# Turning rows by 32x32 blocks on VectorE and carrying the blocks by SBUF copies, in an RWKV-5 attention with a SoLU feed-forward

## The chip, the cores and the metric

The kernel runs on one core of a Trainium2 chip. Its five engines work side by side and meet at semaphores: TensorE (PE; its weight loads are shown as PEld), VectorE (DVE), ScalarE (ACT), GpSimd (POOL) and SyncE (SP), which here issues nearly all DMAs. Each engine takes its instructions strictly in the order in which the program lists them. The metric is the device time of one launch in microseconds. The profile is of one execution.

## The reference

Inputs are r, k and v of shape (4 batches, 8 heads, 768 steps, 48), a decay w and a bonus u of shape (8, 48), and the feed-forward weights w_in (384 x 1024) and w_out (1024 x 384), both in 8-byte floats, with a gain g_ln of 1024.

```python
for t in range(S):
    kt, vt, rt = (k[:, :, t], v[:, :, t], r[:, :, t])
    cur = np.einsum('bhd,bhe->bhde', u[None] * kt, vt)
    y[:, :, t] = np.einsum('bhd,bhde->bhe', rt, state + cur)
    state = w[None, :, :, None] * state + np.einsum('bhd,bhe->bhde', kt, vt)
...
h = x @ w_in                       # x: y as 3072 rows of 384
e = np.exp(h - h_max)
solu = h * (e / e.sum())
ln = (solu - mu) / np.sqrt(var + 1e-06) * g_ln
return ln @ w_out
```

## The kernel before

**Units.** The 3072 rows are 24 units of 128 rows, unit i being batch i % 4 and chunk i // 4 of 128 steps. The recurrence is worked by chunks: within a unit as products of r, k and v with a mask, and between the chunks of one batch through a carried state.

**Stages of a unit.** They are functions that each issue instructions on several engines:

- `load(i, "kr")`, `load(i, "v")` bring the rows in (SP). `decay_k`, `decay_r` and `weigh` multiply them with tables of decays on POOL (L722, L729, L735, L736), into `kp`, `rp` and `rku`; `sum_own` sums `rku` on DVE; `diagonal` writes the diagonal of the score matrix `G` on POOL (L755).
- The scores need r and k turned, features on partitions: `rT` and `kT`. Units below 9 (`FIRST`) are turned by TensorE (`turn_r`, `turn_k`). From unit 9 on it goes through a DMA: `halve_k` and `halve_r` split 4-byte words into lower and upper 2-byte halves on ACT (L1038, L1044; a few on DVE), `turn` issues one transposing DMA on SP (L1012), which turns 2-byte elements only, and `join_rk` puts the halves together again on DVE (L1017).
- `attend` multiplies the scores (L820) and the outer products for the state (L903); `place` copies parts of `rT` into `G` on ACT (L772, L773); `take` moves scores and states out of PSUM on DVE (L833, L924); `merged_y` (L876) and `take_y` give the attention's output; `update` carries the state on (DVE L939, then POOL L942).
- `ffn_in` multiplies with w_in (L952) and takes the exponential on ACT (L957). Its PSUM tile `h_ps` is there once, so the next `ffn_in` waits until `unit_a` (DVE L962, L964) has read it. `unit_b` takes the sum of squares on ACT (L972 from unit 4, `SEVEN`, on), `deviation` makes scale and shift of it on POOL (L984 to L992), and `normalise` applies them on ACT (L998).
- The rows must be turned again for w_out, into `lnT`, with the same three steps: `halve_ln` (ACT L1023), the DMA, `join_ln` (DVE L1017).
- The product with w_out is plain for units 0 to 3 (`ffn_out`, L1062). From unit 4 on two units share seven block products instead of eight: `row_sums_12` and `row_sums_34` form sums s1 to s4 of halves of `lnT` (DVE L1097, L1098; DVE or POOL L1102, L1103). `both_a` has three blocks: two from `lnT` itself, one from s2. `both_b` has three, from s1, s3 and s4, and `both_c` one from `lnT` of the second unit. A block is eight matmul instructions (L1107). Two PSUM accumulators are used in turn; between blocks ACT copies (L1124, L1135, L1140, L1166) or DVE adds (L1133, L1151, L1155) must read them. In `both_b` the copy of L1140 stands between the block from s1 and the block from s4, which use the same accumulator.

**Order.** The whole order of work is written out by hand. After a start for units 0 to 2, a loop over i = 2 to 6 does one unit per turn; a stretch for i = 7 follows; then a loop over i = 9, 11, ..., 23 does two units per turn: attention of units i and i+1, the first product of units j = i-2 and j+1, the second product of units l = i-7 and l+1 (by blocks from l = 4 on), and the loads, decays and turns of units ahead. Three last stretches follow, for l = 18, 20 and 22. The weights come as 14 pieces of 8-byte floats, are rebuilt as 4-byte floats in the first loop, and are loaded and examined again later (`check_next`, from i = 15 on) for a flag that chooses a general path, not taken here.

**The turn of rows around the change.** Within a pair's turn POOL begins with `deviation(j - 2, j)`, for the two units of the turn before; then come the diagonals, row_sums_34, and the decays. `normalise`, `halve_ln` and `join_ln` are spread over ACT's and DVE's order one unit at a time. The split halves and the raw weights share six buffers. `lnT` has two buffers, and the last six units use parts of `big`.

Of the kernel before, what the change touches and what calls it, by code (L numbers as in the profile page):

```python
# [399 lines left out]
def direct_path(  # L400
# [29 lines left out]
    nc = tc.nc  # L430
# [10 lines left out]
    LA, LO, FIRST, WHOLE, CHECKED = 2, 5, 9, 4, 15  # L441
    SEVEN, EARLY, ON_ACT = 4, 12, 12
    ROOM = {18: 4, 19: 5, 20: 3, 21: 2, 22: 1, 23: 0}
# [72 lines left out]
    raws = {}  # L516

    def load_weights(j, tag="raw", bufs=6):
        dst, src, _ = pieces[j]
        raws[j] = wpool.tile([128, dst.shape[1], 2], U32, tag=tag, name="raw", bufs=bufs)  # L520
        n = dst.shape[1]
        n = n if tag == "raw" or j >= 5 else n // 2
        for at in range(0, dst.shape[1], n):
            nc.sync.dma_start(out=raws[j].rearrange("p n o -> p (n o)")[:, 2 * at : 2 * (at + n)],
                              in_=src[:, 2 * at : 2 * (at + n)])
# [53 lines left out]
    def check_words(j):  # L579
# [48 lines left out]
    bigs = [const.tile([128, 8 * T], F32, name=f"big{i}") for i in range(6)]  # L628
# [131 lines left out]
    def factors(i):  # L760
        X = live.setdefault(i, {})
        n = TURNED[i % 3] if i < WHOLE else 2 - i % 2
        X["rk"] = bigs[n].rearrange("p (e a t) -> p e a t", e=2, a=HP)
        X["rT"], X["kT"] = X["rk"][:, 0], X["rk"][:, 1]
        return X

    def place(i):

        X = live[i]
        for q in range(2):  # L770
            rows = slice(q * P, q * P + D)
            nc.scalar.copy(out=X["G"][P : P + D, 0, :, q, :], in_=X["rT"][rows, :, 0:U])  # L772
            nc.scalar.copy(out=X["G"][0:D, 1, :, q, :], in_=X["rT"][rows, :, U:T])  # L773
# [33 lines left out]
    def scores(chunks, at=0):  # L807
# [4 lines left out]
        for n, i in enumerate(chunks, at):  # L812
# [3 lines left out]
            for a in range(HP):  # L816
                for c in range(2):
                    for q in range(2):
                        rows = slice(q * P, q * P + D)
                        nc.tensor.matmul(X["scores"][q][ts(c, U), a, :], X["kT"][rows, a, ts(c, U)],  # L820
                                         X["rT"][rows, a, ts(c, U)], start=True, stop=True)
# [179 lines left out]
    def halves():  # L1001

        return wpool.tile([128, 2 * 8 * 64, 1], U32, tag="raw", name="halves",
                          bufs=6).bitcast(U16).rearrange("p n o -> p (n o)")

    def split(words):
        return words.bitcast(U16).rearrange("p (n o) -> p o n", o=2)

    def turn(both):

        turned = halves()
        nc.sync.dma_start(out=turned.rearrange("p (n t) -> p n t", t=128), in_=both,  # L1012
                          transpose=True)
        return turned.rearrange("p (o n t) -> p o n t", o=2, t=128)

    def join(words, turned):
        nc.vector.tensor_copy(out=words.bitcast(U16).rearrange("p n (t o) -> p o n t", o=2),  # L1017
                              in_=turned)

    def halve_ln(i):  # L1020
        X = live[i]
        both = halves()
        nc.scalar.copy(out=both.rearrange("p (o n) -> p o n", o=2), in_=split(X["solu"]))  # L1023
        X["turned"] = turn(both)

    def join_ln(i):
        X = live[i]
        if i not in ROOM:
            X["lnT"] = fpool.tile([128, KF, 128], F32, name="lnT")
        else:  # L1030
            X["lnT"] = bigs[ROOM[i]].rearrange("p (f t) -> p f t", f=KF)
        join(X["lnT"], X["turned"])

    def halve_k(i):
        X = live[i]
        X["both"] = halves()
        parts = X["both"].rearrange("p (o e n) -> p o e n", o=2, e=2)
        nc.scalar.copy(out=parts[:, :, 1], in_=split(X["kp"].rearrange("p h d -> p (h d)")))  # L1038

    def halve_r(i):  # L1040
        X = live[i]
        parts = X["both"].rearrange("p (o e n) -> p o e n", o=2, e=2)
        copy = nc.vector.tensor_copy if i < ON_ACT else nc.scalar.copy
        copy(out=parts[:, :, 0], in_=split(X["rp"].rearrange("p h d -> p (h d)")))  # L1044
        X["turned"] = turn(X["both"])

    def halve_rk(i):
        if FIRST <= i < N:
            halve_k(i)
            halve_r(i)  # L1050

    def join_rk(i):
        X = factors(i)
        join(X["rk"].rearrange("p e a t -> p (e a) t"), X["turned"])
# [34 lines left out]
    def turn_next(i):  # L1089
        normalise(i)  # L1090
        halve_ln(i)
# [186 lines left out]
    for i in range(LA, LA + LO):  # L1278
# [22 lines left out]
        if i - LO >= 0:  # L1301
            halve_ln(i - LO)
        if i - LO - 1 >= 0:
            join_ln(i - LO - 1)
# [22 lines left out]
        halve_rk(i + 3)  # L1327
# [3 lines left out]
    def check_next():  # L1331
        for p in checked:
            check_words(p)
        checked[:] = [checks.pop(0)] if checks else []
        for p in checked:
            load_weights(p, "check", 1)
# [13 lines left out]
    deviation(0, j)  # L1350
    ffn_in(j)
    halve_k(i + 3)
    attend([i + 1], 1)
    unit(j)
    halve_r(i + 3)
    place(i + 1)
    join_ln(l + 1)
# [7 lines left out]
    halve_ln(l + 2)  # L1365
    join_rk(i + 2)
    ffn_out(l)
    load(i + 6, "kr")
    ffn_in(j + 1)
    unit_a(j + 1)  # L1370
# [3 lines left out]
    join_rk(i + 3)  # L1374
# [5 lines left out]
    halve_rk(i + 4)  # L1380
    unit_b(j + 1)
    halve_ln(l + 3)
    normalise(l + 4)
    join_ln(l + 2)
# [3 lines left out]
    for i in range(LA + LO + 2, N, 2):  # L1388
        j, l = i - LA, i - LA - LO
        seven = l >= SEVEN  # L1390
        for n in (i + 6, i + 7):
# [5 lines left out]
        deviation(j - 2, j)  # L1397
        first, second = ([n] if n < N else [] for n in (i + 2, i + 3))
        for n in first + second:
            diagonal(n)  # L1400
# [199 lines left out]
```

## Time and profile before

| what | value |
|---|---|
| median of 3 runs | 326.86 us (326.11 to 326.93) |
| the profiled execution | 325.9 us, span 324.2 us |
| mean granted clock of TensorE | 0.996 |
| ACT splits of solu (L1023), 24 | 45.5 us, 1896 ns each |
| ACT splits of kp and rp (L1038, L1044) | 15.5 and 12.5 us |
| DVE joins (L1017), 21 and 18 | 33.5 and 30.4 us |
| transposing DMAs, 39 | 4.9 us from issue to landing (median) |
| DMA queue of SP | packets take 84.2% of 16 engines' span; 158302 of 165780 packets under 512 B |

The span is the time from the first to the last instruction. Busy time of an engine counts the time in which it works on an instruction, and a group's mean is the time of one instruction. "Idle before" is the time in which the engine had nothing to do ahead of the group, with what ended that wait. The chain of waits starts from the last instruction and goes back, at each step to whatever released it; it shows which work set the time. The timeline gives instructions by their start in the span.

### The profile page before, as it was taken

To read this page: it belongs to the slowest core of one execution; us is meant where nothing else is said; L and a number is where in the kernel's file an instruction comes from. 1 tells how busy PE (TensorE), PEld (TensorE's weight loads), DVE (VectorE), ACT (ScalarE), POOL (GpSimd) and SP (SyncE) were. 2 spreads that over 40 slices of the span, in tenths; PEclk is the share of its full clock that TensorE was granted. 3 is DMA by queue.
4 is the path that set the end of the run, shared out by engine and by line. 5 is a ranking of instruction groups with operands and counts; after the bars stand their busy time and mean duration, and the time that the engine had idled before them with its cause. 6 is when DMAs were issued, how large, how long until landed. Compare 5 with 4: busy or idle time off the path is not lost.

```text
span 324.2 us, 9670 instructions
## 1 busy us (share of the span) xinstructions
PE 311.9 (96%) x3915; PEld 217.4 (67%) x3915; DVE 255.2 (79%) x434; ACT 244.1 (75%) x414; POOL 220.1 (68%) x237
## 2 busy tenths in 40 slices
PE   8999999999999999899999999999999999999993
PEld 6766556555556457477678667668668667678993
DVE  7796999998887979988798587988579675284571
ACT  5876887988469888768968969959967958957520
POOL 5989778799999999999999999969134020131000
PEclk9999999999999999999999999999999999999998
DMA  7999999689999999986998999978993383873621
GB/s 155 231 276 204 200 207 190 109 141 160 199 165 168 181 198 121 163 175 112 167 181 186 180 193 217 199 185 129 182 197 66 90 191 76 149 169 70 174 80 61
DMA packets 165780, 52.62 MB, mean 162 GB/s; under 512 B 158302, under 2 KB 161503, under 8 KB 165727
## 3 DMA queue, kind: packets, MB, share of 16 engines
q1 hardware_dynamic: 165724, 51.92, 84.2%
q8 instruction: 32, 0.52, 0.7%
q14 instruction: 22, 0.17, 0.2%
q10 hardware_dynamic: 2, 0.00, 0.0%
HBM read 26.75 MB, written 4.72 MB: 97 GB/s over the span
## 4 chain that ended last, share of the span: by engine, by line
PE 53%; DVE 16%; POOL 14%; issue 6%; DMA 4%; ACT 4%; SPq 1%; POOLq 0%; DVEq 0%
PE o_ps L1107 24%; PE h_ps L952 20%; PE y_ps L876 4%; DMA rpad<-in_r_dram 4%; POOL rp L729 3%; POOL big L755 3%; POOL kp L722 3%; POOL rku L735 3%; DVE ma L552 2%; DVE big L833 2%; PE at L820 2%; DVE solu L964 2%; DVE ma L550 1%; PE kv_ps L903 1%; POOL rku L736 1%
## 5 line engine op out<-in xcount | busy, mean ns | idle before, releaser
L952 PE MATMUL h_ps<-w_in_sb,xT 128*128 128x512 f32 x288 | 129.7, 599 | 0.2 <-POOL w_in_sb L560 0.2
L952 PEld LDWEIGHTS h_ps<-w_in_sb,xT 128*128 128x128 f32 x288 | 53.1, 190 | 60.7 <-issue 56.6
L1023 ACT COPY halves<-solu 128x2048 uint16<-128x2048 uint16 x24 | 45.5, 1896 | 0.2
L984 POOL TENSOR_SCALAR stats<-stats 128x2 f32<-128x2 f32 (+2 forms) x12 | 6.2, 520 | 49.8 <-ACT e L972 49.3
L1017 DVE COPY lnT<-halves 128x2048 uint16<-128x2048 uint16 x18 | 30.4, 1702 | 6.2 <-DMA halves<-halves 6.2
L957 ACT ACTIVATE e<-h_ps 128x1024 f32<-128x1024 f32 x24 | 24.5, 1021 | 12.8 <-PE h_ps L952 12.6
L722 POOL TENSOR_TENSOR kp<-kpad,kdec 128x512 f32<-128x512 f32 x24 | 32.6, 1360 | 1.9 <-DMA kpad<-in_k_dram 1.3
L1017 DVE COPY big<-halves 128x2048 uint16<-128x2048 uint16 x21 | 33.5, 1599 | 0.3
L964 DVE SCALAR_TENSOR_TENSOR solu<-h_ps,stats,e 128x1024 f32<-128x1024 f32 x24 | 30.8, 1283 | 2.1
L755 POOL TENSOR_SCALAR_AFFINE_SELECT big<-own 64x512 f32<-64x512 f32 x40 | 29.8, 745 | 1.7
L736 POOL TENSOR_TENSOR rku<-rku,rpad 128x384 f32<-128x384 f32 x24 | 29.1, 1214 | 1.9
L833 DVE COPY_PREDICATED big<-later_half,at 64x512 f32<-64x512 uint32 x40 | 29.5, 738 | 0.7
L735 POOL TENSOR_TENSOR rku<-kpad,u_bc 128x384 f32<-128x384 f32 x24 | 29.0, 1210 | 0.1
L1107 PE MATMUL o_ps<-w_out_sb,ma 128*128 128x192 f32 x160 | 28.3, 328 | 0.1
L998 ACT ACTIVATE solu<-solu,stats 128x1024 f32<-128x1024 f32 x20 | 24.7, 1235 | 4.2 <-POOL stats L992 4.2
L942 POOL TENSOR_TENSOR vt<-vt,wide 48x384 f32<-48x384 f32 x16 | 20.2, 1277 | 9.8 <-DVE vt L939 9.2
L1107 PEld LDWEIGHTS o_ps<-w_out_sb,ma 128*128 128x128 f32 x160 | 26.1, 190 | 0.9 <-ACT o L1140 0.4
L962 DVE RECIPROCAL stats<-sums 128x1 f32<-128x1 f32 x24 | 3.8, 156 | 28.5 <-ACT e L957 28.4
L729 POOL TENSOR_TENSOR rp<-rpad,rdec 128x512 f32<-128x512 f32 x15 | 25.2, 1678 | 0.0
L972 ACT ACTIVATE e<-solu,stats 128x1024 f32<-128x1024 f32 x20 | 22.9, 1145 | 1.4 <-DVE solu L964 1.1
L1062 PE MATMUL o_ps<-w_out_sb,lnT 128*128 128x384 f32 x64 | 21.6, 491 | 0.0
L876 PE MATMUL y_ps<-big,vt 128*32 128x64 f32 (+1 forms) x1280 | 20.7, 220 | 0.4 <-issue 0.4
(148 smaller groups left out, 610.9 us busy)
## 6 DMA issues: line engine op xcount, KB each, us to landing
raw<-in_moe_w_out_dram SPq DMA_DIRECT2D x16, 384.0 KB, 3.8
kpad<-in_k_dram SPq DMA_DIRECT2D x24, 192.0 KB, 5.0
rpad<-in_r_dram SPq DMA_DIRECT2D x24, 192.0 KB, 5.3
vt<-in_v_dram SPq DMA_DIRECT2D x40, 96.0 KB, 3.9
out_dram<-o SPq DMA_DIRECT2D x20, 192.0 KB, 3.5
raw<-in_moe_w_in_dram SPq DMA_DIRECT2D x7, 512.0 KB, 6.7
raw<-in_moe_w_in_dram SPq DMA_DIRECT2D x10, 256.0 KB, 3.3
vt<-in_v_dram SPq DMA_DIRECT2D x4, 192.0 KB, 6.7
```

The lines of the kernel that those rows point to most:

```text
L722: nc.gpsimd.tensor_mul(X["kp"].rearrange("p h d -> p (h d)"), kpads[i % NLD].rearrange("p h d -> p (h d)"), kdec.rearrange("p a d -> p (a ...
L729: nc.gpsimd.tensor_mul(X["rp"].rearrange("p h d -> p (h d)"), rpads[i % NLD].rearrange("p h d -> p (h d)"), rdec.rearrange("p a d -> p (a ...
L735: engine.tensor_mul(rku, kpads[i % NLD][:, :, 0:D], u_bc)
L736: engine.tensor_mul(rku, rku, rpads[i % NLD][:, :, 0:D])
L755: nc.gpsimd.affine_select(out=G[rows, c].rearrange("p a q u -> p (a q) u"), in_=X["own"][rows].to_broadcast([U, H, U]), compare_op=ALU.is_ ...
L833: nc.vector.copy_predicated(X["G"][rows, c].rearrange("p a q u -> p q a u"), later_half[rows].unsqueeze(1).to_broadcast([U, 2, HP, U]), X[ ...
L876: nc.tensor.matmul(y_ps[ts(g, 32), j, ts(c, U)], vf[:, at : at + 32], X["G"][rows, c, h // 2, h % 2, :], start=(g not in opened), stop=las ...
L952: nc.tensor.matmul(h_ps[:, ts(n, NX)], X["xT"][:, j, :], w_in_sb[:, j, ts(n, NX)], start=(j == 0), stop=(j == KD - 1))
L964: nc.vector.scalar_tensor_tensor(out=solu, in0=X["h"], scalar=rs, in1=X["e"], op0=ALU.mult, op1=ALU.mult, accum_out=tot)
L1017: nc.vector.tensor_copy(out=words.bitcast(U16).rearrange("p n (t o) -> p o n t", o=2), in_=turned)
L1023: nc.scalar.copy(out=both.rearrange("p (o n) -> p o n", o=2), in_=split(X["solu"]))
L1107: nc.tensor.matmul(dst, rows[:, f], weights[:, f], start=(start and f == 0), stop=(f == KH - 1), skip_group_check=True)
```

## The change

Rows no longer pass through 2-byte halves and the transposing DMA.

- `turn_ln(i)` and `turn_rk(i)` turn 32x32 blocks of 4-byte words with VectorE's transpose: one instruction of 1024 elements a partition for ln, two of 512 for r and k of a unit. A block stays on its 32 partitions. The results go to `block_ln` and `block_rk`.
- `move` carries the blocks between the four groups of 32 partitions by 16 plain SBUF-to-SBUF copies on SP, each 32 partitions by 256 words of one or two units. `move_ln` and `move_rk` do it for two units at once (one at a time for ln of units 0 and 1, and for r and k of unit 23).
- In the new layout consecutive rows (t) of `lnT`, and of r and k from unit 9 on, lie 8 words apart. The scores, `place`, the row sums and the blocks read them so.
- `deviation` now takes units j-1 and j of the same turn, behind `unit_b(j)`; two `normalise` stand around `ffn_in(j + 1)`.
- The raw weights get eight fixed slots, which the blocks and `lnT` use later. The weight check is split into `check_load` and `check_words` and starts at i = 11.
- In the last stretch `row_sums_12` stands behind `both_a`'s first two blocks.

```diff
-    LA, LO, FIRST, WHOLE, CHECKED = 2, 5, 9, 4, 15
-    SEVEN, EARLY, ON_ACT = 4, 12, 12
-    ROOM = {18: 4, 19: 5, 20: 3, 21: 2, 22: 1, 23: 0}
+    LA, LO, FIRST, WHOLE, CHECKED = 2, 5, 9, 4, 11
+    SEVEN, EARLY = 4, 12
...
+    slots = const.tile([128, 8, 8 * T], F32, name="slots")
+    block_ln, rows_ln, block_rk = slots[:, 6:8], (slots[:, 0:2], slots[:, 2:4]), slots[:, 4:6]
...
+            X["rk"] = bigs[n].rearrange("p (g t e a) -> p e a g t", g=4, e=2, a=HP)
+            X["r"], X["k"] = X["rk"][:, 0], X["rk"][:, 1]
...
-                        nc.tensor.matmul(X["scores"][q][ts(c, U), a, :], X["kT"][rows, a, ts(c, U)],
-                                         X["rT"][rows, a, ts(c, U)], start=True, stop=True)
+                        nc.tensor.matmul(X["scores"][q][ts(c, U), a, :], X["k"][rows, a, ts(c, 2)],
+                                         X["r"][rows, a, ts(c, 2)], start=True, stop=True)
...
+    def move(dst, src):
+        for m in range(4):
+            for g in range(4):
+                nc.sync.dma_start(out=dst[ts(m, 32), :, ts(g, 256)], in_=src[ts(g, 32), :, ts(m, 256)])
+
+    def places_ln(i):
+        dst = rows_ln[i // 2 % 2] if i < N - 4 else big[:, 4:6] if i < N - 2 else big[:, 1:3]
+        return block_rk if N - 4 <= i < N - 2 else block_ln, dst
+
+    def turn_ln(i):
+        nc.vector.transpose(
+            out=places_ln(i)[0][:, i % 2].rearrange("p (m t f) -> p f m t", m=4, f=KF),
+            in_=live[i]["solu"].rearrange("p (f m x) -> p f m x", m=4, f=KF))
+
+    def move_ln(i, n=2):
+        src, dst = places_ln(i)
+        for k in range(i, i + n):
+            live[k]["lnT"] = dst[:, k % 2].rearrange("p (m f) -> p f m", f=KF)
+        move(dst[:, i % 2 : i % 2 + n], src[:, i % 2 : i % 2 + n])
+
+    def turn_rk(i):
+        for e, x in enumerate((live[i]["rp"], live[i]["kp"])):
+            nc.vector.transpose(
+                out=block_rk[:, 1 - i % 2].rearrange("p (m t e a) -> p e a m t", m=4, e=2, a=HP)[:, e],
+                in_=x.rearrange("p h d -> p (h d)").rearrange("p (a m x) -> p a m x", a=HP, m=4))
+
+    def move_rk(i):
+        for n in (i, i + 1):
+            if n < N:
+                factors(n)
+        n = min(2, N - i)
+        move(big[:, 1 : 1 + n], block_rk[:, 0:n])
```

The loop over pairs after the change, in its order (calls that stand as before are cut to the names that the text uses):

```python
for i in range(LA + LO + 2, N, 2):
    j, l = i - LA, i - LA - LO
    ...
    for n in first + second:             # units i+2, i+3
        diagonal(n)
    turn_ln(l + 2)
    turn_ln(l + 3)
    if i >= CHECKED:
        check_load()
    move_ln(l + 2)
    for n in first + second:
        turn_rk(n)
    decay(i + 4)
    decay(i + 5)
    if seven:
        row_sums_12(l)
        row_sums_34(l, nc.vector if l > EARLY else nc.gpsimd)
    ...
    ffn_in(j)
    attend([i, i + 1])
    unit_a(j)
    if seven:
        both_a(l)
    ...
    if first:
        move_rk(i + 2)
    unit_b(j)
    deviation(j - 1, j + 1)
    take([i, i + 1])
    ...
    normalise(l + 4)
    ffn_in(j + 1)
    normalise(l + 5)
    if seven:
        both_b(l)
    unit_a(j + 1)
    if seven:
        both_c(l)
    check_least()
    ...
```

Its last stretch:

```diff
     l += 2
-    both_a(l)
+    both_a(l, (0, 1))
     take_a(l, "DVE")
+    row_sums_12(l)
+    both_a(l, (2,))
     take_a(l, "ACT")
-    check_least()
     compare_sums()
     row_sums_34(l, nc.vector)
```

## The prediction

> **What bounds the kernel now.** I read the page's busy times first, then a table of six stretches, then the chain of waits inside one pair of units, then single lines. One number answers most of it:
>
> ```profile
> PE 311.9 (96%) x3915; PEld 217.4 (67%) x3915; DVE 255.2 (79%) x434; ACT 244.1 (75%) x414; POOL 220.1 (68%) x237
> ```
>
> TensorE is busy 311.9 of 324.2 us. Busy can hide waits, so the table by stretches (columns: length, then busy PE, PEld, DVE, ACT, POOL with counts, clock, DMA share, GB/s) says where the other 12.3 us lie:
>
> ```profile
> 0.00:26.00 26.00, 23.45 (x303) 17.23 (x303) 22.17 (x66) 18.26 (x43) 20.55 (x37) 1.00 0.99 214
> 26.00:67.00 41.00, 38.86 (x620) 24.07 (x624) 37.38 (x68) 33.46 (x65) 33.03 (x35) 1.00 0.94 184
> 67.00:136.00 69.00, 67.34 (x831) 38.65 (x831) 60.65 (x81) 55.26 (x82) 66.19 (x63) 1.00 1.02 165
> 136.00:247.00 111.00, 110.61 (x1600) 80.06 (x1601) 90.28 (x139) 89.47 (x144) 92.57 (x89) 1.00 0.91 171
> 247.00:303.00 56.00, 55.42 (x470) 41.79 (x468) 35.49 (x62) 44.64 (x73) 7.75 (x16) 1.00 0.58 123
> 303.00:324.20 21.20, 16.23 (x98) 15.57 (x98) 9.23 (x23) 3.03 (x10) 0.00 (x0) 0.94 0.36 104
> ```
>
> From 26 to 303 us TensorE idles only 2.14 + 1.66 + 0.39 + 0.58 = 4.8 us. That is the most the change can win there. POOL is almost full from 67 to 136 (66.19 of 69). One pair of units, as the chain of waits has it (start, length, what):
>
> ```profile
> 188.84 1.93 PE y_ps L876 x128
> 190.77 5.35 PE h_ps L952 x12
> 196.11 1.09 PE at L820 x64
> 197.21 0.72 PE kv_ps L903 x64
> 197.93 4.10 PE o_ps L1107 x24
> 202.02 0.03 issue
> 202.05 5.42 PE h_ps L952 x12
> 207.47 5.29 PE o_ps L1107 x32
> ```
>
> All TensorE, back to back, some 23.9 us a pair. Relieving other engines is worth nothing here; delaying TensorE costs in full. Call E the end of the third block of both_b (187.3 here; the next is 1.3 before the 5.29 us stretch ends).
>
> **Part by part, removed.** ACT loses its splits: 45.5 us (24 x 1.896), 15.5 and 12.5 us. VectorE loses the joins, 33.5 + 30.4 us, and 39 transposing DMAs go. In the pairs that is hidden behind TensorE already: price 0. Only POOL gains, through the joins:
>
> ```profile
> L729 POOL TENSOR_TENSOR rp<-rpad,rdec x15: 1264/1288/2338, 69.9 to 211.0; 128x512 f32<-128x512 f32 x15
> L722 POOL TENSOR_TENSOR kp<-kpad,kdec x24: 1267/1277/2347, 9.4 to 209.8; 128x512 f32<-128x512 f32 x24
> ```
>
> Equal products take 1.27 us or up to 2.35 (shortest/median/longest). Setting POOL's rows against VectorE's: the 18 kp products with no join beside them average 1.28 us, the 6 with at least 0.4 us of one 1.61 us. POOL's time over its shortest rows sums to 29.7 us, some 21.6 of it where joins (L1017) overlap. What stays after the change is about 8 us. The Trainium skill, "SBUF — State Buffer", section Who interferes with whom, says a VectorE instruction with one SBUF input outside its two-port modes leaves GpSimd alone; no row here shows a turn. By the page the stall worked out below stays at its middle value; if turns were of the two-port kind it would go to its upper one.
>
> **Added.** VectorE turns: per pair two of 1024 elements and four of 512. No row shows a turn. Bounds: a plain pass at one element a step, 1.28 us per 1024 (L964) and 0.69 per 512 (L780); from above twice that, since writes go 32 bytes apart. I take the rows: 2 x 1.28 + 4 x 0.69 = 5.3 us against 4 joins x 1.65 = 6.6. VectorE has room: about E+10 for row_sums_12, when the exponential of the next unit ends.
>
> SyncE issues 16 copies per move, 13 moves for ln and 8 for r, k: 336 issues for 39. The shortest issues of plain DMAs (L1156) take 0.33 us, with 0.08 between: 0.41, so 6.6 us a move. Per pair: 13.1 for two moves, 2.6 for four k, r loads, 2.8 for four v loads, 2 for checks, 1 for results: 21.5 of 23.9 us. It fits, narrowly; at a k load's 0.57 + 0.08 each it is 29.2 and doesn't. I take 0.41: few rows of 1 KB each are nearest to the output's 128 rows. What is queued behind move_rk (it waits for place) are check_load and the results, none due within 5 us.
>
> Strided operands: lnT and r, k are read by TensorE 32 bytes apart. No row of before does that. Lower bound 0. Upper: the transposes of L787 (a 128-column load and a matmul of 128) run 0.11 us apart, so a load takes no more; doubled it is 0.22 against the 0.163 us between matmuls of L1107. 24 per pair x 0.057 x 10 pairs = 13.7 us, and scores (1.09 us per pair) doubled add 0.545 x 15 units = 8.2: 22 us. I take 0, nearest row: VectorE reads 8 bytes apart (L550, 512 words) in 692 ns, a dense pass of 512 (L780) takes 689. The Trainium skill speaks against it: "SBUF — State Buffer", section Door 1: The DMA port swizzle, has 16-byte lines in SBUF and a penalty for each access that enters a new one, which a step of eight f32 always does. By the rule the sum would hold those 22 us, by the rows 0.
>
> Start to 136 us: POOL regains most of its 13.7 us of slow rows there and VectorE two joins, but TensorE idles only 3.8; i = 5 gets a turn of 1.28 us where VectorE is on the chain and had no join, and i = 7 makes POOL wait for the deviation of a unit just computed, with two diagonals and two decays queued behind. I take -1.2 (bounds -3.8, all of that idle time, and +2, one wait for such statistics).
>
> The weight checks stay 14, but run two a pair from i = 11 on: 0.87 us of ACT (L582 with its accumulator) and 0.6 of VectorE (L590) each. ACT hides its part under TensorE now that it has lost some 8 us of splits a pair (two of 1.90, four of 1.04); VectorE's lies ahead of POOL's start and is counted there. Weights landing in fixed slots cost nothing: the same loads, with more room.
>
> **Moved: the deviation.** Before, POOL computes deviation(j-2, j) first in the pair, on old statistics (193.3 us), and normalise runs on ACT in a free place. After, deviation(j-1, j+1) stands behind diagonal, two whole decays and row_sums_34, and normalise(l+4) stands on ACT ahead of the exponential of ffn_in(j+1), normalise(l+5) behind it, then the copy of both_b. That copy frees the accumulator for TensorE's third block of both_b. From E:
> - POOL starts when VectorE has done o, a check_least (0.6) and two updates: E+1.85. Then, at undisturbed rows, two L942 2.0, four L755 2.8, two decays with their products 9.0, row sums 2.5, deviation 1.4: D = E+19.6. Statistics are ready at E+17.1 (place ends E+15.9, Square 1.2), so POOL ends last.
> - ACT after D: normalise 1.13, exponential 1.03, normalise 1.13, copy 0.3: D+3.7.
> - TensorE: ffn_in(j+1) ends at 207.47, E+20.2; after two blocks of 1.3 it wants the copy at E+22.8.
>
> Stall = D - (E+19.1) = 0.5 us, and 0.5 for the contention that stays (8 us in some ten pairs' time, a little over half of it ahead of the deviation): 1.0 a pair. Four pairs carry the full POOL load (l = 4 to 10; at 12 one decay is left, later none): +4.0. Bounds: 0 if POOL starts a little earlier; with POOL's present 22.7 us a pair D = E+24.5, 5.4 a pair, +22.
>
> **The tail.** Now (start, length):
>
> ```profile
> 293.55 5.21 PE o_ps L1107 x32
> 299.37 1.25 ACT solu L998
> 300.64 1.90 ACT halves L1023
> 303.03 13.31 PE o_ps L1107 x80
> ```
>
> After ffn_in(23) ends at 293.55, twelve blocks of 1.30 us stand before both_a(22): wanted at 309.2. New: normalise ends 300.6, row_sums_12(20) is done by then, turn 1.28 to 301.9, sixteen issues to 308.5, last landing about 1.9 after its issue's start: 310.0. Late 0.8. Then row_sums_12(22), which now runs before both_a (310.6 to 312.0), stands behind take_a: two blocks, then 0.36 + 2 x 0.69 with TensorE idle, 1.8. Tail +2.6 (bounds 0 and +4.5).
>
> **Sum** against the profiled execution's own 325.9 us (span 324.2 and 1.7 around it; 0.96 below the median of runs): 325.9 - 1.2 + 4.0 + 2.6 = 331.3.
>
> **Rivals.**
> - A, faster. Place: POOL. Freed from the joins it ends the deviation before E+19.1, from there no pair stalls, and the 4.8 us of idle are what is won: at best 325.9 - 4.8 = 321.1, with half of it and a short tail 323.6. For: 21.6 us of POOL time. Against: D at undisturbed rows is already 0.5 late, and the tail.
> - B, strided operands cost TensorE: 331.3 + 22 = 353, half of it 342. For: 32 bytes have no like in the trace. Against: the rows at 8.
> - C, SyncE's queue becomes the bound: 29.2 - 23.9 = 5.3 a pair over four pairs with loads: 331.3 + 21 - 4.0 = 348. Against: 0.33 us issues.
> - D, nothing moves, gains and tail cancel: 326.9.
>
> **How the numbers follow.** My forecast has 0.47 (its own range 328 to 339), A 0.26, B 0.14, C 0.06, D 0.07. A measurement here tells 0.3%, about 1 us, from no change. Faster is A, 0.26; same is D, 0.07; slower 0.67. Range 323.5 to 345: half of A, and some of B and C, are left out.
>
> **What would show it.** In pairs with l = 4 to 10: TensorE waiting some 1 us before the last eight matmuls of both_b, released by ACT's copy at L1140's place, and ACT's normalise waiting for POOL's stats. POOL's products near 1.27 us throughout. Matmuls from lnT still 0.163 us apart (0.22 is B). SyncE issues near 0.35 us. At the end about 2 us of TensorE idle before s[2]'s block. If TensorE idles nowhere in the pairs and the page shows some 318 us of span, I am wrong at the deviation; if the matmuls themselves lengthen, at the strides.

## The result, and the profile after

The changed kernel takes 419.2 us (median of 4 runs, 418.84 to 419.58) against 326.72 us (4 runs, 326.11 to 326.93): 1.2835 times the time, 95% interval 1.2812 to 1.2857. The prediction said 331.3, range 323.5 to 345. It had the sign, by two terms (+4.0 and +2.6) that turned out to be the smaller part of the loss, and missed the size.

The first lines of the page of the changed kernel (busy time and share of the span of 417.6 us; then the granted clock of TensorE in 40 slices):

```profile
PE 356.9 (85%) x3915; PEld 266.4 (64%) x3915; DVE 280.5 (67%) x446; ACT 192.5 (46%) x363; POOL 199.2 (48%) x235
...
PEclk9999998967999959899898998988999999999869
```

The table by stretches, with the same columns as before:

```profile
...
26.00:67.00 41.00, 38.94 (x617) 24.00 (x616) 37.46 (x67) 32.23 (x64) 31.86 (x34) 1.00 0.87 179
67.00:84.00 17.00, 15.07 (x186) 10.44 (x186) 11.21 (x16) 4.96 (x10) 14.87 (x17) 0.90 0.37 75
84.00:95.00 11.00, 0.00 (x0) 0.00 (x0) 5.11 (x7) 0.00 (x0) 0.00 (x0) 0.60 0.37 78
95.00:140.00 45.00, 44.79 (x477) 30.94 (x478) 31.66 (x48) 23.53 (x38) 32.42 (x39) 0.95 0.61 122
140.00:340.00 200.00, 169.24 (x1962) 128.42 (x1961) 135.98 (x191) 91.16 (x164) 94.14 (x99) 0.92 0.56 128
...
390.00:417.60 27.60, 16.45 (x67) 15.52 (x66) 6.69 (x17) 1.27 (x4) 0.00 (x0) 0.81 0.19 59
```

Before, TensorE idled 4.8 us from 26 to 303 us. Now it stands still for 11 us at 84 and for 31 of the 200 us from 140 on, and in those stretches the clock (third column from the end) is below 1.00; in the kernel before it was so only in the last stretch (0.94). The waits of TensorE of the changed kernel (what it waited for, us in total, times, longest) say at which places:

```profile
PE at L834 <- DMA big<-slots: 15.7, 9, 4.7
PE o_ps L1101 <- ACT o L1134: 13.8, 7, 3.1
PE h_ps L966 <- DVE solu L978: 11.4, 1, 11.4
PE o_ps L1101 <- DMA big<-slots: 3.8, 1, 3.8
...
PE o_ps L1101 <- DVE ma L1092: 2.9, 1, 2.9
```

The first is the scores waiting for the copies of r and k, the second both_b's last block (predicted, at 4.0 in all), the third one stall at 84 us that nothing in the prediction has, and the last two are the tail (6.6 together, 2.6 predicted). The chain through the tail:

```profile
393.44 2.06 DMA big<-slots
...
395.70 5.21 PE o_ps L1101 x16
...
401.43 1.09 DVE ma L1091
...
402.54 1.09 DVE ma L1092
...
403.77 5.80 PE o_ps L1101 x24
```

TensorE begins both_a(22) when the last copy of lnT has landed, does two blocks, and waits again for two row sums.

The longer span, 417.6 - 324.2 = 93.4 us, can be divided in three. Cut into stretches of 1 us, the busy time of TensorE times (1 - granted clock) sums to 20.2 us, and to 0.0 before. So **idle time** grew by 60.7 - 12.3 = 48.4, **20.2 were lost to a lowered clock**, and at full clock TensorE was busy 356.9 - 20.2 - 311.9 = **24.8 us longer for the same 3915 matmuls**. The last figure is a remainder. The same subtraction leaves 5.9 us in e1_dense (below), whose operands lie as before, so by itself it is good to some 6 us.

Why the pairs idle is seen in the chain of waits of the changed kernel inside one pair (start, length, what):

```profile
204.18 0.75 SPq L1020
...
216.21 0.59 SPq L1020
...
217.48 3.77 DMA raw<-in_moe_w_in_dram
...
222.61 0.66 SPq L528
...
227.27 1.94 DMA slots<-slots
229.21 2.08 POOL ma L1096
...
237.68 0.21 ACT o L1134
...
238.03 2.01 PE o_ps L1101 x10
```

Before, such a chain was TensorE from end to end, 23.9 us a pair, and SyncE's issues were 1% of the whole kernel's chain; after, they are 23%. Now the pair is SyncE issuing copy after copy (L1020), with a wait for a weight check's load (L528) in between, and then POOL and ACT; TensorE turns up only at the end. From 202 to 273 us the pairs take 35.9 and 34.7 us. The copies' line, as one answer of the trace of the changed kernel has it (shortest/median/longest issue in ns), beside the v loads' line of the kernel before:

```profile
L1020 SPq DMA_DIRECT2D slots<-slots x176: 512/595/1581, 62.9 to 356.3; - x176
```

```profile
L480 SPq DMA_DIRECT2D vt<-in_v_dram x44: 434/627/4256, 4.7 to 225.5; - x44
```

An issue of a copy takes 0.595 us and the next starts 0.04 later: 0.635, where the prediction took 0.41. In the pair from 202.1 to 238.0 us SyncE's 46 issues of all kinds add up to 29.5 us, or 31.4 with the 0.04 behind each; the prediction had 21.5. Rows of that size stood in the trace of before.

### The profile page after: what moved, and what is told of

Its sections match the earlier page's. It is cut to its first block, busy times and chain, and to the rows that moved or that the text cites. A ratio compares the mean times of both kernels' runs of the same rounds, so it can differ in the third digit from the quotient of the medians.

```text
span 417.6 us, 10095 instructions
## 1 busy us (share of the span) xinstructions
PE 356.9 (85%) x3915; PEld 266.4 (64%) x3915; DVE 280.5 (67%) x446; ACT 192.5 (46%) x363; POOL 199.2 (48%) x235
## 4 chain that ended last, share of the span: by engine, by line
PE 24%; SPq 23%; DVE 14%; POOL 13%; issue 9%; ACT 8%; DMA 8%; DVEq 0%; ACTq 0%; POOLq 0%
SPq L1020 18%; PE o_ps L1101 13%; PE h_ps L966 7%; PE y_ps L890 2%; DVE slots L1039 2%; POOL rp L737 2%; SPq L479 2%; ACT solu L1012 2%; POOL rku L743 2%; ACT e L971 2%; POOL ma L1096 1%; DMA big<-slots 1%; ACT big L786 1%; DVE slots L1027 1%; DMA slots<-in_moe_w_out_dram 1%
## 5 line engine op out<-in xcount | busy, mean ns | idle before, releaser
L966 PE MATMUL h_ps<-w_in_sb,xT 128*128 128x512 f32 x288 | 133.3, 612 | 11.9 <-DVE solu L978 11.4
L1027 DVE STREAM_TRANSPOSE slots<-solu 128x1024 f32<-128x1024 f32 x24 | 47.6, 2041 | 12.4 <-DMA slots<-slots 11.3
L786 ACT COPY big<-big 48x256 f32<-48x256 f32 x80 | 47.6, 595 | 1.4
L1101 PE MATMUL o_ps<-w_out_sb,ma 128*128 128x192 f32 x160 | 32.5, 351 | 13.8 <-ACT o L1134 13.8
L737 POOL TENSOR_TENSOR rp<-rpad,rdec 128x512 f32<-128x512 f32 x15 | 23.3, 1557 | 32.0 <-DVE slots L1039 31.3
L834 PE MATMUL at<-big 48*64 48x64 f32 x640 | 24.6, 285 | 15.7 <-DMA big<-slots 15.7
L834 PEld LDWEIGHTS at<-big 48*64 48x64 f32 x640 | 21.3, 192 | 24.5 <-DMA big<-slots 12.2
L1039 DVE STREAM_TRANSPOSE slots<-rp 128x512 f32<-128x512 f32 x15 | 16.6, 1105 | 30.2 <-DMA big<-slots 30.2
L730 POOL TENSOR_TENSOR kp<-kpad,kdec 128x512 f32<-128x512 f32 x24 | 34.0, 1417 | 5.9 <-DMA kpad<-in_k_dram 4.9
L589 ACT ACTIVATE mag<-raw 128x384 f32<-128x384 f32 (+1 forms) x14 | 8.6, 614 | 59.0 <-DVE slots L1039 18.9
L956 POOL TENSOR_TENSOR vt<-vt,wide 48x384 f32<-48x384 f32 x16 | 13.0, 829 | 45.7 <-DVE vt L953 45.4
L1101 PE MATMUL o_ps<-w_out_sb,slots 128*128 128x192 f32 x128 | 33.7, 419 | 0.0
L986 ACT ACTIVATE e<-solu,stats 128x1024 f32<-128x1024 f32 x20 | 22.9, 1145 | 21.5 <-DVE solu L978 21.3
L1101 PEld LDWEIGHTS o_ps<-w_out_sb,slots 128*128 128x128 f32 x128 | 31.8, 335 | 0.6
L847 DVE COPY_PREDICATED big<-later_half,at 64x512 f32<-64x512 uint32 x40 | 29.5, 737 | 0.6
```

Source lines behind the costliest of these rows:

```text
L730: nc.gpsimd.tensor_mul(X["kp"].rearrange("p h d -> p (h d)"), kpads[i % NLD].rearrange("p h d -> p (h d)"), kdec.rearrange("p a d -> p (a ...
L737: nc.gpsimd.tensor_mul(X["rp"].rearrange("p h d -> p (h d)"), rpads[i % NLD].rearrange("p h d -> p (h d)"), rdec.rearrange("p a d -> p (a ...
L786: nc.scalar.copy(out=X["G"][to, c, :, q, :].rearrange("p a (g t) -> p a g t", g=2), in_=X["r"][rows, :, 2 * c : 2 * c + 2])
L834: nc.tensor.matmul(X["scores"][q][ts(c, U), a, :], X["k"][rows, a, ts(c, 2)], X["r"][rows, a, ts(c, 2)], start=True, stop=True)
L847: nc.vector.copy_predicated(X["G"][rows, c].rearrange("p a q u -> p q a u"), later_half[rows].unsqueeze(1).to_broadcast([U, 2, HP, U]), X[ ...
L966: nc.tensor.matmul(h_ps[:, ts(n, NX)], X["xT"][:, j, :], w_in_sb[:, j, ts(n, NX)], start=(j == 0), stop=(j == KD - 1))
```

## The experiments

Each is one run with its profile, beside one run of the kernel before on the same chip (326.2 to 327.1 us in all of them). Line numbers shift by a few from kernel to kernel. Kernels that leave copies out, keep blocks from crossing or read words in another order (e2, e3, e5, e6, e7, e9, e12, e15, e16) give other values than the reference; they are run for their time. "Theory Q" below is the queue of copies, "S" the strides.

### Strides or copies

**e1_dense** is the changed kernel with rows one word apart again; the 16 copies of a move stay, in runs of 128 bytes.

```diff
-            out=places_ln(i)[0][:, i % 2].rearrange("p (m t f) -> p f m t", m=4, f=KF),
+            out=blocks(places_ln(i)[0])[:, :, i % 2].rearrange("p m f t -> p f m t"),
...
-                nc.sync.dma_start(out=dst[ts(m, 32), :, ts(g, 256)], in_=src[ts(g, 32), :, ts(m, 256)])
+                nc.sync.dma_start(out=to[ts(m, 32), :, ts(g, 32)], in_=at[ts(g, 32), m])
```

> The changed kernel with rows one word apart again: blocks are turned to (f, t) and carried in runs of 128 bytes, still 16 copies a move. Theory S (strides): operands 32 bytes apart cost TensorE 0.157 us in each of 240 matmuls from lnT (0.320 apart against 0.163) and 0.5 us in the scores of 15 units, 45 us in all, and lengthen turns (2.04 us), place (0.60) and row sums; then this run falls from 419 to about 370 us or less, with matmuls from lnT 0.163 us apart, turns near 1.2 us and place near 0.40 us. Theory Q (SyncE's queue): 32 issues a pair of 0.595 + 0.04 us are the bound (29 us a pair against 23.9), strides lie beside it; then the time stays above 400 us. I expect something between, about 385, because both act.

**e2_wide** keeps the strides, and carries lnT of two units with 4 copies of 128 partitions, which take nothing across the groups.

```diff
+        if wide:
+            for g in range(4):
+                nc.sync.dma_start(out=dst[:, :, ts(g, 256)], in_=src[:, :, ts(g, 256)])
+            return
```

> The changed kernel, strides kept, but the moves of ln for two units are 4 copies of 128 partitions instead of 16 of 32, so that blocks stay on their partitions (the crossing of lnT's blocks is left out, the output isn't the reference's). SyncE's issues per pair fall from 32 to 20, some 7.6 us less. Theory Q: the queue is no longer the bound (about 21 us a pair), the time falls to what the strides leave, 326 + 45 + tail, about 375 us. Theory S alone: the queue was hidden behind slow matmuls, the time stays within 8 us of 419.

**e3_dense_wide** has both edits.

> Both at once: rows one word apart, and 4 wide copies for the moves of ln (the crossing of lnT's blocks is left out). If strides and queue together are the whole loss, what is left is the order of the work (deviation behind POOL's decays, tail): 327 to 340 us, with TensorE waiting about 1 us a pair before the last block of both_b. Over 350 says that a third cause is at work.

Measured: 421.4, 379.2 and 355.5 us. Without the strides nothing is won while the copies are there (+2.2, where I had expected some 34 less), and 23.8 us once they are fewer; fewer copies for lnT alone win 40.0 and, without strides, 65.9. So each hides beside the other, and the copies are the outer bound. e2_wide carries the same bytes for lnT as before, 4 copies of 256 KB in place of 16 of 64 KB, so it is the number of issues that counts, not the bytes. e3_dense_wide is above what I expected of it: a third cause is left.

**e4_stride** leaves the kernel before as it is, but the joins write their words 32 bytes apart.

```diff
-        nc.vector.tensor_copy(out=words.bitcast(U16).rearrange("p n (t o) -> p o n t", o=2),
+        nc.vector.tensor_copy(out=words.bitcast(U16).rearrange("p (t n o) -> p o n t", o=2, n=8),
```

> The kernel before with nothing changed but the layout its joins write: lnT, and r and k from unit 9 on, 32 bytes apart, as in the changed kernel. No turns by blocks, no copies. Theory S: TensorE alone loses 38 us in the blocks and 8 us in the scores, 326 + 45 = about 371 us, more if place (0.60 against 0.40 us) or the joins become late. If the time stays under 340, strides were not what cost the changed kernel its time.

Measured: 445.0 us, and no clean price of the weight loads: the joins themselves went from 1.6 and 1.7 us to 5.1 and 5.3, and VectorE became the bound (busy 90% of the span). **e5_stride_read** therefore leaves the joins alone and only reads apart.

```diff
+        X["apart"] = X["lnT"].rearrange("p f t -> p (f t)").rearrange("p (t f) -> p f t", f=KF)
...
-            nc.tensor.matmul(o_ps, X["lnT"][:, f, :], w_out_sb[:, f, :],
+            nc.tensor.matmul(o_ps, X["apart"][:, f, :], w_out_sb[:, f, :],
```

> The kernel of before, its joins dense as they were; only TensorE's blocks read lnT through a view whose neighbours stand 32 bytes apart (same bytes, other order, so the values of these blocks are mixed up). Theory S (the strides cost TensorE): 240 matmul records with a weight load from lnT go from 0.163 to 0.32 us apart, +37.7 us, 326.3 + 37.7 = 364, 357 to 368 with some of it covering idle time. Rival Q (the weight load lies beside other work): 326 to 330. VectorE's joins stay at 1.6 to 1.7 us, POOL's rows too.

Measured: 340.1 us, +13.9, between the two theories, and TensorE 16.8 us longer busy. Weight loads by form (busy us, mean ns), of this kernel:

```profile
L1108 PEld LDWEIGHTS o_ps<-w_out_sb,lnT 128*128 128x128 f32 x112 | 27.3, 335 | 0.4
L1108 PEld LDWEIGHTS o_ps<-w_out_sb,ma 128*128 128x128 f32 x160 | 26.2, 190 | 0.1
```

A load from rows 32 bytes apart takes 335 ns, a dense one 190. The matmuls behind it start 0.24 us apart where they were 0.163: 240 x 0.077 = 18.5. I had expected 0.32, read off stretches of the changed kernel in which the clock was halved. The price of lnT's strides is 16.8 us; what is left of the 24.8 is 8.0 for r and k in the scores (and e2_wide, with little lost clock, has 342.7 - 4.1 - 311.9 = 26.7 in all). The scores of one pair at full clock, in the kernel before and then in e2_wide, say nearly the same:

```profile
196.04 1.16 PE L820 MATMUL at<-big 48*64 48x64 f32 x64
```

```profile
168.65 2.19 PE L834 MATMUL at<-big 48*64 48x64 f32 x64
```

That is 1.03 us for two units, 7.7 for fifteen.

### The third cause

**e6_norm_late** is e3_dense_wide with the two `normalise` behind both_b's copy; **e7_front** adds another buffer for the turned blocks of units 0 and 1; **e9_few** leaves out 12 of the 16 copies of r and k as well.

```diff
-        normalise(l + 4)
         ffn_in(j + 1)
-        normalise(l + 5)
         if seven:
             both_b(l)
+        normalise(l + 4)
+        normalise(l + 5)
...
-        return block_rk if N - 4 <= i < N - 2 else block_ln, dst
+        return rows_ln[1] if i < 2 else block_rk if N - 4 <= i < N - 2 else block_ln, dst
...
+                if m == g or not few:
+                    nc.sync.dma_start(out=to[ts(m, 32), :, ts(g, 32)], in_=at[ts(g, 32), m])
```

> e3_dense_wide with one more edit: normalise(l+4) and normalise(l+5) stand behind both_b's copy on ACT, not around the exponential ahead of it (lnT's crossing is still left out). Theory D (the wait before both_b's last block is the late deviation, through normalise): the five waits of 1.46 to 3.29 us there, 10.0 in sum, fall under 2 in sum, and 355.4 becomes 346 (344 to 349). Rival (ACT or POOL is late as a whole, so that the wait turns up before lnT's blocks or the scores): no less than 352.

> e6_norm_late with one more edit: units 0 and 1 turn into another buffer (the rows that units 2 and 3 move to later), so that the turns of units 2 and 3 don't wait for the single moves of 0 and 1. Theory F (the gap of 11.2 us before h_ps at 92 us is VectorE standing in a turn that waits for these copies): the gap falls under 2 us, the time by 9 to 11 against e6_norm_late, to 335 to 338. Rival (SyncE's queue, with 32 single issues and the next move behind them, holds the same place): the gap moves to lnT or stays, under 4 us gained.

> e7_front with 12 of the 16 copies of each move of r, k left out too (only the blocks that stay in their 32 partitions are carried; the others hold r, k of earlier units). Theory Q2 (what holds e7_front at 352 is a ring through SyncE's queue: 16 issues of r, k end so late that the next pair's turns wait for them 33 us in sum, POOL and the scores behind them): the DVE wait of turns on copies falls under 5 us, TensorE's idle time from 28.4 to 12 to 16 us, its busy time at a lowered clock from 6.2 to under 2, and 352.0 becomes 330 to 336, near before. Rival (ACT, POOL or the order of the pair hold it): 344 or more.

Measured: 355.6, 352.0 and 329.3 us. In e6_norm_late the waits before both_b's last block do vanish, but the scores' waits for copies of r and k come up at once (6.0 us by TensorE's waits); the same pair, another place, no gain. In e7_front the stall of 11.4 us falls to 2.9 and only 3.6 us are won: the scores' waits for copies grow to 7.6 us, and TensorE's idle time falls by 5.8 us only. Then e9_few takes 22.7 us away in one step. TensorE's busy time in it and its longest waits:

```profile
PE 311.7 (95%) x3915; PEld 220.1 (67%) x3915; DVE 236.5 (72%) x446; ACT 178.0 (54%) x363; POOL 187.6 (57%) x235
```

```profile
PE o_ps L1063 <- DVE solu L974: 3.2, 1, 3.2
...
PE o_ps L1108 <- DVE ma L1099: 1.9, 1, 1.9
```

TensorE is busy 311.7 us, as before (311.9), and idle 15.9 instead of 60.7. Dense rows, fewer copies and the two moved waits account for the change down to 2.9 us (329.34 against 326.46). The two waits above, what is left of the stall at the front (3.2) and the row sums of the tail (1.9), are more than that. So the turns by VectorE, the new places of the checks and the freed POOL, gains against losses, show no cost of their own.

**e12_few_only** asks whether the two waits outside the queue are real, or its echo: e3_dense_wide with few copies of r and k, and nothing moved.

> e3_dense_wide with 12 of the 16 copies of each move of r, k left out as in e9_few; normalise and the single moves of units 0 and 1 stand as the change has them. This is the changed kernel with a SyncE queue that isn't bound in the pairs and no strides, so it shows the two other steps alone. Theory D (the moved deviation makes TensorE wait whatever the queue does, as the prediction has it): waits before both_b's last block of 4 to 10 us in sum, and with the front gap of 11 us and some lowered clock behind it 343 to 350. Theory Q3 (those waits were the queue's too: it made turns, decays and POOL late): under 2 us in sum there, the front gap stays, 337 to 342.

Measured: 348.8 us, theory D. The timeline of this kernel around one both_b (start, length, what, and the wait before it):

```profile
171.45 1.29 POOL L1104 TENSOR_TENSOR ma<-slots,ma 128x512 f32<-128x512 f32 x1
172.69 0.21 POOL L994 TENSOR_SCALAR stats<-stats 128x2 f32<-128x2 f32 x1
...
174.06 0.19 POOL L1002 TENSOR_TENSOR stats<-stats 128x2 f32<-128x2 f32 x1
174.28 1.24 ACT L1008 ACTIVATE solu<-solu,stats 128x1024 f32<-128x1024 f32 x1 [1.51 <-POOL stats L1002]
175.43 1.00 ACT L967 ACTIVATE e<-h_ps 128x1024 f32<-128x1024 f32 x1
176.43 1.23 ACT L1008 ACTIVATE solu<-solu,stats 128x1024 f32<-128x1024 f32 x1
177.56 0.30 ACT L1141 COPY o<-o_ps 128x192 f32<-128x192 f32 x1
178.00 0.56 PE L1108 MATMUL o_ps<-w_out_sb,ma 128*128 128x192 f32 x2 [1.80 <-ACT o L1141]
```

This is the predicted chain, link by link: POOL ends its row sums and the deviation, then ACT has normalise, exponential, normalise and the copy, and TensorE has waited 1.80. Four pairs have it (0.89, 1.80, 1.79, 1.79: 6.3 us).

### The price of a copy, or a ring of waits

**e15_eight** and **e16_twelve** are e1_dense with 8 and 12 copies a move.

```diff
+                if (m ^ g) < 3 if rk else g < 2:
+                    nc.sync.dma_start(out=to[ts(m, 32), :, ts(g, 32)], in_=at[ts(g, 32), m])
+                elif not rk and m < 2:
+                    nc.sync.dma_start(out=to[ts(m, 64), :, ts(g, 32)], in_=at[ts(m, 64), g])
```

> e1_dense with 8 copies in each move instead of 16 (half of the blocks are left out or not taken across, as in e9_few and e2_wide; the single moves too); nothing else is changed. Theory P (the pair is bound by the issues' sum): 16 x 0.635 + 8.5 = 18.7 us a pair fits in 23.9, so this is e12_few_only (348.8 with 4 a move in the pairs) less a part of its front gap: 338 to 352. Theory R (a ring from turn to copies to scores and back to the turn, to which every copy adds its time, full or not): on the line from 348.8 at 4 to 421.4 at 16, 365 to 380.

> e1_dense with 12 copies in each move. Theory P: 24 x 0.635 + 8.5 = 23.7 us a pair, just full against TensorE's 23.9, so that only SyncE's waits (some 3 to 5 us a pair) show: 355 to 385. Theory R: on the line, 390 to 405.

Measured: 343.5 and 373.2 us, both in the range of theory P. From 4 to 8 copies a move the time hardly changes: 348.8 and 343.5, or 337.3 and 340.8 without the stall at the front (11.5 us in the first, 2.7 in the second, whose single moves of units 0 and 1 have 8 copies in place of 16). From 8 to 12 it rises by 29.7 us, from 12 to 16 by 48.2, each time for 21 moves x 4 = 84 more issues: 0.35 and 0.57 us an issue. Not all of the 48.2 is SyncE's time: 14.1 are clock lowered behind the longer waits (22.5 us against 8.4, by the sum used above), and 4.5 are the front again (11.4 against 6.9). So an issue is free up to 8 copies and dear from 12 on; the price begins somewhere between, and at 16 it comes near an issue's length with what follows from it.

**e13_checks_act** takes the loads of the weight checks out of SyncE's queue, **e14_dense_checks** does so in the dense kernel with the edits of e7_front.

```diff
-            load_weights(checked[0], "check", 1)
+            load_weights(checked[0], "check", 1, nc.scalar)
```

> The changed kernel with one edit: the loads of the weight checks are issued from ACT's queue instead of SyncE's. In the changed kernel's chain of waits a pair of 34 us has 28.5 us of SyncE issues and some 5 us in which SyncE stands before the second check load (one buffer, still being read), with the next pair's copies behind it. Theory W (that wait is a part of the queue's bound of its own): 4 to 6 us less a pair in five to seven pairs, 419 becomes 385 to 400. Theory P (the issues' price alone sets the pair, the wait only fills a hole): 410 or more.

> Nothing left out: all copies on SyncE, rows one word apart, normalise behind both_b's copy, units 0 and 1 turned into another buffer, and the check loads issued from ACT's queue. What is left against before is then the price of 32 issues a pair (28.5 us of issues less 1.0 for the checks, against 23.9 us of TensorE). Theory W: 3.6 us in eight pairs, 355 to 370. Theory P: 385 or more.

Measured: 427.8 and 459.0 us; theory W falls. SyncE's waits in e13_checks_act:

```profile
SPq L479 <- DMA raw<-in_moe_w_in_dram: 13.0, 3, 4.8
SPq L1020 <- DMA raw<-in_moe_w_out_dram: 12.2, 4, 4.0
```

SyncE now stands before a v load or a copy until the check's load has landed, though neither uses its data: the wait only moved. Why an unrelated issue waits for it I have not settled. That e14_dense_checks is 37.6 us worse than e1_dense I didn't foresee. The same kind of wait stands in its trace, longer:

```profile
SPq L1021 <- DMA raw<-in_moe_w_out_dram: 30.7, 7, 6.0
SPq L1021 <- DMA raw<-in_moe_w_in_dram: 16.3, 4, 5.9
```

With those before other loads SyncE stands 64.4 us until a check's load has landed, where in e1_dense it stood 18.9 us, and that before the check loads alone; the scores wait 90.9 us for copies of r and k. No run separates this from the other edits of e14_dense_checks.

### Other ways to carry the blocks

**e8_dram** carries the blocks through DRAM in 8 issues a move, **e10_act_queue** issues all copies of r and k from ACT, **e11_two_queues** half of them (the second diff). All three have dense rows and the edits of e7_front.

```diff
+            nc.sync.dma_start(out=far.rearrange("x m n g t -> x (m n) g t")[:, :, g, :],
+                              in_=at[ts(g, 32)].rearrange("p (n t) -> p n t", t=32))
...
+            nc.sync.dma_start(out=to[ts(m, 32)], in_=far[:, m].rearrange("x n g t -> x (n g t)"))
```

```diff
+                queue = nc.scalar if rk and g % 2 else nc.sync
+                queue.dma_start(out=to[ts(m, 32), :, ts(g, 32)], in_=at[ts(g, 32), m])
```

> The edits of e7_front, but nothing left out: the turned blocks, rows one word apart, go to a scratch in DRAM in four copies (one for each group of 32 partitions, 128-byte runs) and come back in four of 32 partitions with whole rows, 8 issues a move in place of 16, for lnT and for r, k. Theory (the queue is what bound the changed kernel, and with at most 8 x 0.64 = 5.1 us a move it isn't bound): 333 to 345. Rival (the way through DRAM, two landings of 2 us or more and runs of 128 bytes, makes lnT or r, k late in each pair): 350 or more, with waits of PE on copies.

> Nothing left out: the changed kernel with rows one word apart, all 16 copies a move, normalise behind both_b's copy, units 0 and 1 turned into another buffer, and the moves of r, k issued from ACT's queue, those of lnT from SyncE's. Theory Q2: SyncE has 16 x 0.635 + 8.5 = 18.7 us a pair and fits in 24; ACT has some 12.3 + 10.2 = 22.5 of 24: 332 to 348 by how often ACT's place in the order is late. Rival (the two queues slow each other, an issue of 1.2 us in each): 380 or more.

> e10_act_queue with the 16 copies of r, k taken in turn by SyncE and ACT, 8 each: SyncE 24 x 0.635 + 8.5 = 23.7 us a pair, ACT 12.3 + 5.1 = 17.4. Theory Q2: the copies of r, k are done 5 us earlier than from one queue, but SyncE is full: 336 to 350. Rival (queues slow each other): 380 or more.

Measured: 446.4, 412.5 and 389.7 us, all three in the ranges of the rivals. Through DRAM the scores wait 79.7 us for copies: SyncE stands until the first half of a move has landed, 66.7 us in all, some 3.2 a move, with all else behind it. From ACT's queue an issue takes 0.64 us against 0.63 on SyncE's, so the rivals' reason, queues that slow each other, isn't what is seen; but ACT then waits ahead of the Square of `unit_b`, which POOL's deviation waits for. Waits of ACT in e10_act_queue:

```profile
ACT e L982 <- DMA vt<-in_v_dram: 52.3, 4, 14.5
...
ACT e L982 <- DMA big<-slots: 33.5, 3, 13.3
```

Two queues are the best of the versions that carry every block (389.7), and still 63 us behind the kernel before. None found here beats it. No run has the edits of e7_front with every block carried by SyncE and the checks where the change has them; the nearest is e1_dense (421.4).

## Why the prediction was wrong, point by point

- **SyncE's queue: the step that failed.** The prediction took "0.33 us, with 0.08 between: 0.41", because "few rows of 1 KB each are nearest to the output's 128 rows", and had 21.5 us of 23.9. A copy's issue is 0.595 + 0.04. That is rival C's price (0.57 + 0.08), given 0.06. C's sum of 29.2 us a pair is near the measured 31.4. Even C was short in all: 5.3 us over four pairs, where two measured pairs grew by 12.0 and 10.8 us and the step from 12 to 16 copies costs 0.57 us an issue counted over all moves, since SyncE's own waits (3.8 us for a check's load in the chain above) and the waits behind it add to the sum of issues. The trace of before had plain DMAs with a median issue from 0.33 us (the last results) to 0.74 (the r loads); the shortest was taken as the nearest, by a likeness of row counts that decides nothing: in the runs a copy's issue takes 0.6 to 0.7 us with 32, 64 or 128 partitions.
- **The check loads.** The prediction counted them as "none due within 5 us" and overlooked that the next pair's copies are queued right behind them. e13_checks_act shows that taking them away there doesn't help by itself.
- **Strided operands: taken as 0, measured 24.8 us.** The upper bound was right to 3 us: 13.7 for lnT (16.8 measured) and 8.2 for the scores (8.0 as the remainder, 7.7 read directly). The choice of the low end failed: a VectorE read at 8 bytes apart says nothing of a weight load at 32. The Trainium skill ("SBUF — State Buffer", section Door 1: The DMA port swizzle) says that each access into a new 16-byte line pays; loads of 335 against 190 ns agree with it, and the measurement adds the factor, which the page doesn't give: the 22 us that the prediction set beside the page's rule came from its own doubling. A step of 32 bytes also costs VectorE (the turn of 1024 takes 2.04 us strided, 1.22 dense) and ACT (`place` 595 and 403 ns), off the path here.
- **The start: -1.2 forecast, a stall of 11.4 us found.** The prediction followed POOL and missed VectorE: the turn of units 2 and 3 writes blocks that the 32 single copies of units 0 and 1 still read, and `unit_a`, which frees `h_ps` for TensorE, is behind it in VectorE's order. The timeline of the changed kernel:

```profile
89.77 2.02 DVE L1027 STREAM_TRANSPOSE slots<-solu 128x1024 f32<-128x1024 f32 x1 [11.33 <-DMA slots<-slots]
...
93.75 1.28 DVE L978 SCALAR_TENSOR_TENSOR solu<-h_ps,stats,e 128x1024 f32<-128x1024 f32 x1
...
95.09 2.93 PE L966 MATMUL h_ps<-w_in_sb,xT 128*128 128x512 f32 x3 [11.37 <-DVE solu L978]
```

- **The moved deviation: mechanism right, size off.** In e12_few_only POOL starts 1.9 us after E (1.85 forecast), ends the deviation at E+20.3 (19.6), the copy ends 3.6 later (3.7), and TensorE wants it at E+22.2 (22.8). The stall is 1.8 us a pair, not 1.0, 6.3 in the four pairs named. In the changed kernel the full queue stretches it to 13.8.
- **The tail: right places, too small.** Forecast 0.8 for lnT and 1.8 for the row sums, found 3.8 and 2.9. Sixteen issues at 0.635 instead of 0.41 are 3.6 us more; the row sums take 1.09 us strided instead of 0.69. With dense rows and few copies the second wait is 1.9.
- **What was removed: right.** POOL's busy time falls by 20.9 us (21.6 forecast) and ACT's by 51.6, and in e9_few, with strides and most copies out of the way, that buys no time: rival A had nothing to win by. "POOL's products near 1.27 us throughout" holds beside the turns, which the prediction had to leave open: in the changed kernel every decay product (L730, L737) with a turn beside it takes 1.27 to 1.30 us. The slow ones, 1.99 to 2.15, all stand beside a VectorE instruction with two operands in SBUF: `row_sums_12` (L1091, L1092) or, once, a sum of weights (L1081). So rp averages 1.56 us there, and 1.27 in e12_few_only.
- **The lowered clock: no term at all.** 20.2 us follow from the waits, not from the change itself.

## What to carry to other kernels

Count a queue in issues, not in bytes, and price an issue from its own kind of transfer in the trace; when the sum comes near the length of a stage, the longest of the near rows decides, not the shortest. A layout that an engine off the path can write cheaply may be dear for TensorE's weight loads: price it by the load. And where a wait for a buffer's old readers stands ahead of work on an engine's list, everything behind it waits too, however idle that engine is on average.

## What was not expected of the hardware

A stall of TensorE costs more than its length. The changed kernel around the stall from 84 to 95 us, by windows (the clock is the third number from the end):

```profile
84.00:88.00 4.00, 0.00 (x0) 0.00 (x0) 0.00 (x0) 0.00 (x0) 0.00 (x0) 0.79 0.18 50
88.00:92.00 4.00, 0.00 (x0) 0.00 (x0) 2.23 (x2) 0.00 (x0) 0.00 (x0) 0.50 0.64 115
92.00:96.00 4.00, 0.91 (x1) 0.50 (x2) 3.87 (x7) 0.87 (x1) 0.00 (x0) 0.50 0.31 78
...
98.00:100.00 2.00, 2.00 (x4) 0.82 (x3) 1.42 (x3) 0.64 (x2) 1.85 (x3) 0.51 0.39 100
100.00:102.00 2.00, 2.00 (x6) 0.88 (x5) 0.00 (x0) 0.00 (x0) 2.00 (x3) 1.00 0.39 98
```

TensorE's last matmul before the stall ends at 83.7 us; 0.79 over the first window puts the fall to half clock near 86.3. It works again from 95.1 on, but at half clock until about 100. Waits of a few microseconds in the pairs did the same: around one of 4.7 us for copies the clock is 0.50 from 145 to 154 us. The Trainium skill ("TensorE: Matmul & The Clock Gate", section What's actually happening) describes this: half clock after an idle window of some 3.4 us, full clock after as much sustained work. The windows agree in the ratio; the fall came sooner here, some 2.6 us after the last matmul, and the return took nearer 5. Over the whole kernel it made 48.4 us of idle time into 68.6.
